# Routing attention and its feed-forward block on one core: loads dealt out two a slot, and GpSimd's indirect transfers held by a matmul

## The chip, the core and the metric

The kernel runs on one core of a Trainium2 chip. Six things work at once on that core, each with its own queue of instructions, taken in order: TensorE (PE in the profile; PEld is its loading of weights), VectorE (DVE), ScalarE (ACT), GpSimd (POOL), SyncE (SP, which here only issues transfers), and the core's 16 DMA engines, which carry the transfers out. An instruction names the semaphore values that it waits for; until they are there, everything behind it in its queue stands too. The metric is the device time of one execution in microseconds (us); lower is better.

## The reference

```python
def _attn_ref(q, k, v, centroids):            # 4 batches, 8 heads, 768 tokens, 64 wide
    q_assign = np.argmax(np.einsum('bhsd,hcd->bhsc', q_n, c_n), axis=-1)   # 16 clusters
    k_assign = np.argmax(np.einsum('bhsd,hcd->bhsc', k_n, c_n), axis=-1)
    mask = q_assign[:, :, :, None] == k_assign[:, :, None, :]
    scores = scale * np.matmul(q, k.transpose(0, 1, 3, 2))
    scores = np.where(mask, scores, -1000000000.0)
    attn = softmax(scores)                    # written out in the original
    return np.matmul(attn, v)

def _moe_ref(x, w_in, w_out, alpha):          # x: 3072 tokens by 512
    h = x @ w_in                              # 512 by 2048
    g = np.maximum(h, 0.0) + alpha * np.minimum(h, 0.0)
    return g @ w_out                          # 2048 by 512
```

A query attends only to the keys of its own cluster; q_n, k_n and c_n are q, k and the centroids divided by their norms. The heads' results side by side are x.

## The kernel before

The unit of attention is a pair: two heads of one batch. There are 16 pairs, n = 0 to 15. Pairs 0 to 8 score all keys against all queries and mask. Pairs 9 to 15 are sorted by cluster first: GpSimd scatters their rows of q, k and v to a scratch tensor in DRAM in the order of the clusters (order_scatter, an indirect transfer whose row numbers lie in the tile off), SyncE reads them back sorted (order_load), only blocks near the diagonal are scored, and GpSimd scatters the results back to the tokens' own order (put_back), from where SyncE fetches them (fetch_back).

Time goes by steps, u = 0 to 74. The steps up to 23 are the first part. From step 24 on (the second part, from about 195 us; 51 steps to about 800 us, so 12 us each on average) each pair or half pair has three steps, s = 0 to 2. A step has five slots; in the first step of a pair the score and weigh block (score, invert, weigh or weigh_near, mask, normalise, score again) takes the place of the first three, and two slots follow. In each slot the code writes out, in this order: tick (pieces that have come due: put_back is one), one piece of the attention's sums, the scatters that scatters_at allows, feed (one product of the feed-forward block, taken from the deque ffn: hidden, L1079, or final, L1097), and prepare (the work for later pairs: order_features, order_blocks and others). This order of the code is the order of each engine's queue. The pieces of ffn are what TensorE does between two blocks.

Two things set when transfers start. A load (load, load_v, order_load, fetch_back) is written out whole at the start of its step: eight transfers of 96 KB for q and k of a pair (tile qk), one or two for v (tile vt). SyncE issues them as soon as their buffer is free. GpSimd's indirect transfers (168 scatters, L688, and 84 put-backs, L1024) are paced by a handed number: pace() writes a 1x1 copy into ScalarE's queue (L664, tile pace, 8 buffers) and a 1x1 copy of that into GpSimd's (L665), so that GpSimd gets there only when ScalarE has come to that place in its own queue. A slot's scatters have one such pair of copies ahead of the first, each put-back has one of its own.

The scatters read their rows from two stage tiles in turn, which order_stage (L674) fills from q, k and v by three transfers on SyncE's queue, once the scatters of the tile's last use are done.

Of the kernel before, what the change touches and what calls it, by code (L numbers as in the profile page):

```python
# [23 lines left out]
def kernel(  # L24
# [77 lines left out]


    pairs = [(b, hp) for b in range(B) for hp in range(NCH)]
    NO = WHOLE * NCH - 3
# [9 lines left out]
    def load(n):  # L115

        b, hp = pairs[n]
        for w, src in enumerate((q, k)):  # L120
            raw = inp.tile([P, 2, NJ, D], FP32, name="qk")
            if n < 2:
                nc.sync.dma_start(
                    out=raw.rearrange("p h j d -> p h (j d)"),
                    in_=src[b, 2 * hp:2 * hp + 2].rearrange("h (p j) d -> p h (j d)",
                                                            j=NJ))
            elif n < NCH:
                for h in range(2):
                    nc.sync.dma_start(
                        out=by_token(raw)[:, :, h * D:(h + 1) * D],  # L130
                        in_=src[b, 2 * hp + h].rearrange("(p j) d -> p j d", j=NJ))
            for h in range(2):
                rows = src[b, 2 * hp + h]
                for x in range(D // Q if n >= NCH else 0):
                    r = h * D + x * Q
                    nc.sync.dma_start(
                        out=raw.rearrange("p h j d -> p (h j d)")[r:r + Q, :].rearrange(
                            "p (t i) -> p t i", i=Q),
                        in_=rows[:, x * Q:(x + 1) * Q].rearrange("(t p) i -> p t i", p=Q))
            raw_qk[n, w] = raw  # L140

    def load_v(n):
# [3 lines left out]
        if n < NCH:  # L146
            nc.sync.dma_start(out=vt.rearrange("p h j d -> p h (j d)"),
                              in_=rows.rearrange("h (p j) d -> p h (j d)", j=NJ))
        else:
            nc.sync.dma_start(out=vt.rearrange("p h j d -> p (h j) d"),  # L150
                              in_=rows.rearrange("h (j p) d -> p (h j) d", p=P))
        vts[n] = vt

# [353 lines left out]
    def second_part():  # L507

        first_part.close()
        for name, bufs in (("emore", 1), ("ordc", 1), ("ordp", 1), ("order", NP - NO),  # L510
                           ("xmore", 1), ("byrow", 1), ("pace", 8)):
            sorts[name] = fast.enter_context(tc.tile_pool(name=name, bufs=bufs))
# [3 lines left out]
    def order_constants():  # L516
# [23 lines left out]
        shift = ordc.tile([P, 2], FP32, name="shift")  # L540
        sorts["paced"] = ordc.tile([1, 1], FP32, name="paced")

# [136 lines left out]
    def order_scatter(n, i, x):  # L679
# [8 lines left out]
        nc.gpsimd.indirect_dma_start(  # L688
            out=scratch[n][1][h * NX + xx],
            out_offset=bass.IndirectOffsetOnAxis(ap=ranks[n][:, xx, h:h + 1], axis=0),  # L690
            in_=sorts["stage"][i % STAGES][:, x, :], in_offset=None,
            element_offset=h * 2 * S * P)

    def order_load(n):
# [3 lines left out]
            "p (h j d) -> p h j d", h=2, d=1)  # L698
        for h in range(2):
            r0 = 2 * h * S  # L700
            nc.sync.dma_start(out=found[:, h], in_=whole.bitcast(I32)[
                r0:r0 + S, D:D + 1].rearrange("(j p) d -> p j d", p=P))
        orders[n] = found
        for w in range(2):
            raw = inp.tile([P, 2, NJ, D], FP32, name="qk")
            for h in range(2):
                r0 = (2 * h + w) * S
                for x in range(D // Q):
                    r = h * D + x * Q
                    nc.sync.dma_start(  # L710
                        out=raw.rearrange("p h j d -> p (h j d)")[r:r + Q, :].rearrange(
                            "p (t i) -> p t i", i=Q),
                        in_=whole[r0:r0 + S, x * Q:(x + 1) * Q].rearrange(
                            "(t p) i -> p t i", p=Q))
            raw_qk[n, w] = raw
        vt = vpool.tile([P, 2, NJ, D], FP32, name="vt")
        for h in range(2):
            r0 = (2 * h + 1) * S
            nc.sync.dma_start(out=vt[:, h], in_=whole[r0:r0 + S, D:2 * D].rearrange(
                "(j p) d -> p j d", p=P))  # L720
        vts[n] = vt

# [298 lines left out]
    def put_back(to, place, rows, i):  # L1021
        j, h = divmod(i, 2)
        pace()
        nc.gpsimd.indirect_dma_start(  # L1024
            out=to[i],
            out_offset=bass.IndirectOffsetOnAxis(ap=place[:, h, j:j + 1], axis=0),
            in_=rows[j // HJ][:, j % HJ, h * D:(h + 1) * D], in_offset=None, element_offset=h * S * D)

    def fetch_back(n, whole):

        b, hp = pairs[n]
        raw = inp.tile([P, 2, NJ, D], FP32, name="qk").rearrange("p h j d -> p (h j d)")
        for h in range(2):
            for x in range(D // Q):
                r = h * D + x * Q
                nc.sync.dma_start(
                    out=raw[r:r + Q, :].rearrange("p (t i) -> p t i", i=Q),
                    in_=whole[h * S:(h + 1) * S, x * Q:(x + 1) * Q].rearrange(
                        "(t p) i -> p t i", p=Q))
# [22 lines left out]
    def ffn_pieces(b, half):  # L1062
# [12 lines left out]
        def hidden(f):  # L1075
            convert_up_to((f // FQ + 1) * (NCH + FQ) - FQ)
            ps = ps_f.tile([P, 512], FP32, name="fps")
            for c in range(NCH):
                nc.tensor.matmul(out=ps[:, 0:HS],  # L1079
                                 lhsT=w_in_sb[:, c, f * P:(f + 1) * P],  # L1080
                                 rhs=xTs[b, half][:, c, :],
                                 start=(c == 0), stop=(c == NCH - 1))
            slopes()
# [6 lines left out]
        def final(i, f0, on, off):  # L1090
# [5 lines left out]
            for f in range(f0, f0 + FQ):  # L1096
                nc.tensor.matmul(out=ps[:, 0:DM], lhsT=gs[f][:, i * P:(i + 1) * P],  # L1097
                                 rhs=w_out_sb[:, f, :], start=on and f == f0,
                                 stop=off and f == f0 + FQ - 1)
            if off:  # L1100
# [427 lines left out]
    todo = deque()  # L1528
    for u in range(TOGETHER, NS + 1):
        for piece in load_at.get(u, []):  # L1530
# [53 lines left out]
        for i in slots:  # L1584
# [19 lines left out]
    assert not prep_at and not todo  # L1604
    while due:
        tick()
        if due:
            tick()
# [222 lines left out]
```

## Time and profile before

| | before |
|---|---|
| median of three timed runs | 960.9 us (960.55 to 964.36) |
| profiled execution | 961.2 us, of which the profile's span is 959.3 |
| TensorE busy | 927.1 us, 97% of the span |
| VectorE, GpSimd, ScalarE busy | 656.2, 385.5 and 261.9 us |
| mean granted TensorE clock | 0.986 of full speed |

The profile is one execution; its time is the span and 1.9 us around it. TensorE's granted clock has two levels, 1.2 and 2.4 GHz, shown as 0.5 and 1.0; a value between them is a mean over a stretch. A time in brackets in a row is the idle time of the engine ahead of that instruction, with what ended it.

### The profile page before, as it was taken

The page shows a single profiled execution, that of the slowest core. Times are in us where ns is not written, and L with a number is a line of the kernel's source. Part 1 is how long each engine was busy: PE and PEld are TensorE (multiplying, and loading weights), DVE is VectorE, ACT ScalarE, POOL GpSimd, SP SyncE. Part 2 cuts the span into 40 slices and gives each one's busy share as a digit, 9 for nine tenths or more (in the row PEclk, how much of TensorE's full clock was granted, in tenths as well). Part 3 has the DMA queues.
Part 4 walks back from the last instruction along what each step waited for, and adds up shares of the span by engine and source line. Part 5 has one row for each costly group of instructions (what it writes and reads, how often), then busy time and mean ns, then how long its engine had stood idle before and what let it go on. Part 6 is the DMA issues. An engine that isn't in the chain of part 4 may idle for free.

```text
span 959.3 us, 11845 instructions
## 1 busy us (share of the span) xinstructions
PE 927.1 (97%) x3891; PEld 496.7 (52%) x3891; DVE 656.2 (68%) x1246; ACT 261.9 (27%) x660; POOL 385.5 (40%) x579
## 2 busy tenths in 40 slices
PE   8899999999999999999899999989899999999997
PEld 5434444445454444454454544545445454556886
DVE  5897798799498678798877988753446244598200
ACT  5664543322123221232223232112203120121000
POOL 2422222210036578477736777657615272000000
PEclk9999999999999999999999999999799999999999
DMA  9433757048002555155824353652421012000000
GB/s 287 141 114 105 146 117 141 17 92 161 0 14 80 138 118 123 39 117 124 164 49 66 51 106 99 135 105 64 70 56 26 11 35 57 1 1 0 23 23 26
DMA packets 231892, 77.71 MB, mean 81 GB/s; under 512 B 216960, under 2 KB 219728, under 8 KB 231824
## 3 DMA queue, kind: packets, MB, share of 16 engines
q1 hardware_dynamic: 222912, 62.72, 30.6%
q0 software_dynamic: 8064, 13.78, 4.5%
q8 instruction: 33, 0.54, 0.2%
q10 hardware_dynamic: 848, 0.39, 0.2%
q14 instruction: 35, 0.29, 0.1%
HBM read 52.25 MB, written 24.25 MB: 80 GB/s over the span
## 4 chain that ended last, share of the span: by engine, by line
PE 88%; DVE 3%; another core or an unknown queue 3%; ACT 2%; issue 2%; DMA 1%; SPq 0%; POOL 0%; ACTq 0%; DVEq 0%; POOLq 0%
PE fps L1079 25%; PE fps L1097 25%; PE sps L797 7%; PE vps L952 6%; PE sps L1315 4%; PE sps L1259 4%; PE fps L797 2%; PE vps L1259 2%; PE vps L1315 2%; PE mps L985 1%; PE fps L1315 1%; PE fps L1259 1%; PE vps L985 1%; PE sps L806 1%
## 5 line engine op out<-in xcount | busy, mean ns | idle before, releaser
L1079 PE MATMUL fps<-xT,w_in_sb 128*128 128x384 f32 x768 | 262.5, 495 | 8.3 <-ACT more L815 6.2
L1097 PE MATMUL fps<-w_out_sb,gT 128*128 128x512 f32 x576 | 254.1, 595 | 0.3 <-DVE gT L1071 0.3
L688 POOL DMA_INDIRECT scratch<-stage,off x168 | 178.4, 1062 | 64.5 <-issue 30.4
L1079 PEld LDWEIGHTS fps<-xT,w_in_sb 128*128 128x128 f32 x768 | 143.8, 192 | 113.6 <-ACT more L815 9.8
L1097 PEld LDWEIGHTS fps<-w_out_sb,gT 128*128 128x128 f32 x576 | 107.5, 190 | 132.2 <-issue 121.9
L665 POOL COPY paced<-pace 1x1 f32<-1x1 f32 x204 | 53.8, 264 | 166.7 <-ACT pace L664 164.7
L1085 ACT COPY gT<-fps 128x384 f32<-128x384 f32 x96 | 45.9, 478 | 240.7 <-PE fps L1079 185.4
L1071 DVE SCALAR_TENSOR_TENSOR gT<-gT,alpha 128x384 f32<-128x384 f32 x96 | 61.5, 649 | 69.1 <-ACT gT L1085 58.3
L1024 POOL DMA_INDIRECT back<-rows,off x84 | 87.0, 1036 | 22.8 <-issue 18.0
L797 PE MATMUL sps<-qkT 64*128 64x384 f32 (+1 forms) x464 | 87.2, 491 | 0.5 <-issue 0.5
L818 ACT ACTIVATE E<-sps 128x768 f32<-128x768 f32 (+1 forms) x76 | 56.4, 787 | 62.7 <-PE sps L806 42.6
L797 PEld LDWEIGHTS sps<-qkT 64*128 64x128 f32 x464 | 42.2, 188 | 39.6 <-issue 16.6
L838 DVE SCALAR_TENSOR_TENSOR more<-aq,key,more 128x384 f32<-128x384 bf16 (+2 forms) x116 | 60.4, 579 | 0.6 <-ACT more L815 0.6
L952 PE MATMUL vps<-E,vt 128*64 128x384 f32 x292 | 54.2, 495 | 0.0
L280 POOL TENSOR_TENSOR w_in_sb<-w_in_sb,power 128x512 f32<-128x512 f32 x16 | 24.0, 1502 | 68.6 <-DVE w_in_sb L277 68.6
L920 DVE RECIPROCAL inverses<-mps 64x12 f32<-64x12 f32 (+1 forms) x42 | 10.5, 251 | 52.9 <-PE mps L907 43.3
L280 POOL TENSOR_TENSOR w_out_sb<-w_out_sb,power 128x512 f32<-128x512 f32 x16 | 22.9, 1430 | 58.3 <-DVE w_out_sb L277 58.3
L838 DVE SCALAR_TENSOR_TENSOR E<-aq,key,E 128x384 f32<-128x384 bf16 (+2 forms) x88 | 45.1, 570 | 0.1
L848 DVE TENSOR_TENSOR acc<-acc,E 128x768 f32<-128x768 f32 x35 | 33.3, 951 | 14.5 <-ACT E L818 13.6
L1103 ACT COPY y<-fps 128x512 f32<-128x512 f32 x18 | 10.5, 586 | 99.2 <-PE fps L1097 86.8
L1105 DVE TENSOR_TENSOR y<-y,fps 128x512 f32<-128x512 f32 x24 | 16.4, 683 | 28.2 <-PE fps L1097 26.2
L797 PE MATMUL fps<-qkT 64*128 64x384 f32 (+1 forms) x136 | 31.0, 501 | 4.3 <-issue 3.6
(288 smaller groups left out, 1179.6 us busy)
## 6 DMA issues: line engine op xcount, KB each, us to landing
raw<-in_moe_w_in_dram SPq DMA_DIRECT2D x16, 512.0 KB
raw<-in_moe_w_out_dram SPq DMA_DIRECT2D x16, 512.0 KB
out_dram<-y SPq DMA_DIRECT2D x21, 256.0 KB
qk<-scratch SPq DMA_DIRECT2D x56, 96.0 KB
qk<-in_q_dram SPq DMA_DIRECT2D x48, 96.0 KB
qk<-in_k_dram SPq DMA_DIRECT2D x48, 96.0 KB
w_in_kept<-w_in_sb SPq DMA_DIRECT2D x8, 512.0 KB
vt<-in_v_dram SPq DMA_DIRECT2D x9, 384.0 KB
```

The costliest lines, as they stand in the source:

```text
L665: nc.gpsimd.tensor_copy(out=sorts["paced"], in_=token)
L688: nc.gpsimd.indirect_dma_start(out=scratch[n][1][h * NX + xx], out_offset=bass.IndirectOffsetOnAxis(ap=ranks[n][:, xx, h:h + 1], axis=0), ...
L797: nc.tensor.matmul(out=bank(ps, h, m), lhsT=qkT[r:r + D, S + c * P:S + (c + 1) * P], rhs=qkT[r:r + D, tokens], start=True, stop=not early_ ...
L818: nc.scalar.activation(out=E[:, :, 0:m], in_=ps[:, :, 0:m], func=AF.Exp, scale=SCALE)
L838: nc.vector.scalar_tensor_tensor(out=e, in0=of, scalar=keys[n][:, NJ + c, h:h + 1], in1=e, op0=ALU.is_equal, op1=ALU.mult)
L952: nc.tensor.matmul(out=po[r:r + D, 0:HS], lhsT=vts[n][:, h, c, :], rhs=e[:, h, :], start=(c == 0), stop=(c == NJ - 1))
L1024: nc.gpsimd.indirect_dma_start(out=to[i], out_offset=bass.IndirectOffsetOnAxis(ap=place[:, h, j:j + 1], axis=0), in_=rows[j // HJ][:, j % ...
L1071: nc.vector.scalar_tensor_tensor(out=gs[f], in0=gs[f], scalar=alpha[:, f:f + 1], in1=gs[f], op0=ALU.mult, op1=ALU.max)
L1079: nc.tensor.matmul(out=ps[:, 0:HS], lhsT=w_in_sb[:, c, f * P:(f + 1) * P], rhs=xTs[b, half][:, c, :], start=(c == 0), stop=(c == NCH - 1))
L1097: nc.tensor.matmul(out=ps[:, 0:DM], lhsT=gs[f][:, i * P:(i + 1) * P], rhs=w_out_sb[:, f, :], start=on and f == f0, stop=off and f == f0 + ...
L1259: nc.tensor.matmul(out=bank[to], lhsT=w_in_form(m, x, cc), rhs=rhs[:, cc, :], start=start and cc == 0, stop=cc == KH - 1, skip_group_check ...
L1315: nc.tensor.matmul(out=bank[to], lhsT=g_form(m, x, t), rhs=w_out_form(n, x), start=start and x == 0, stop=x == NQ - 1, skip_group_check=no ...
```

## The change

It has two parts. First, pace() and its two copies go. Each indirect transfer of GpSimd's waits instead for mark[0], the feed-forward matmul that was written out last; in a slot the scatters stand ahead of feed, so that this is the product of the slot before. Second, in the second part a load isn't written out whole at the start of its step. Its transfers go into a deque, loading, and deal(2) writes out two in each slot, each with a wait for mark[0]. A load counts as there (raw_qk, vts and orders are set) when its last transfer is written out; the row numbers (off) come last of a sorted pair's load, where they were first. turn_back, which reads what fetch_back fetched, comes 5 slots after the last of its transfers was written out, where it came 7 after the whole fetch (3 for 4 in the last pair). The loads of the first part, the stage loads (order_stage), the stores of w_in_kept and those of y are as before.

```diff
+    loading, mark, dealing = deque(), [None], []
+    def dealt(pieces, done):
+        loading.extend((1, piece) for piece in pieces)
+        loading.append((0, done))
+        if not dealing:
+            deal(len(loading))
+    def deal(room):
+        while loading and room >= loading[0][0]:
+            count, piece = loading.popleft()
+            piece()
+            room -= count
+    def paced(ins):
+        tc.add_manual_dep(
+            ins.ins, mark[0].ins.name,
+            mybir.DependencyInfo(mybir.DependencyClass.Sync, mybir.DependencyReason.DATA),
+            reason="paced")
+    def transfer(out, in_):
+        dma = nc.sync.dma_start(out=out, in_=in_)
+        if dealing:
+            paced(dma)
...
-    def pace():
-        token = sorts["pace"].tile([1, 1], FP32, name="pace")
-        nc.scalar.copy(token, ones[0:1, 0:1])
-        nc.gpsimd.tensor_copy(out=sorts["paced"], in_=token)
...
-        nc.gpsimd.indirect_dma_start(
+        paced(nc.gpsimd.indirect_dma_start(
             out=scratch[n][1][h * NX + xx],
...
     def put_back(to, place, rows, i):
         j, h = divmod(i, 2)
-        pace()
-        nc.gpsimd.indirect_dma_start(
+        paced(nc.gpsimd.indirect_dma_start(
...
-        later(4 if n == NP - 1 else 7, turn_back)
+            lambda: later(3 if n == NP - 1 else 5, turn_back))
...
-                nc.tensor.matmul(out=ps[:, 0:HS],
+                mark[0] = nc.tensor.matmul(out=ps[:, 0:HS],
...
             todo.popleft()()
+            deal(2)
             room = scatters_at(u - start_of[NO, None], s, i)
-            if room and sorting:
-                pace()
             while sorting and room:
...
-    while due:
+    while due or loading:
         tick()
+        deal(2)
```

On GpSimd's queue, at the first scatters of the first sorted pair, before: each slot's transfers follow a copy that waits for ScalarE (Activation), and the transfers themselves wait for nothing or for their stage load (the DMAHW semaphores).

```order
L685 COPY stage_1727<-number 64x4
L688 DMA scratch_2118<-stage_1727,off 3072x128 [waits DMAHW6_49,DMAHW7_49,DMAHW5_49,Pool_49]
L665 COPY paced<-pace 1x1 [waits Activation_49]
L688 DMA scratch_2118<-stage_1727,off 3072x128
L665 COPY paced<-pace 1x1 [waits Activation_49,Pool_49]
L688 DMA scratch_2118<-stage_1727,off 3072x128
L665 COPY paced<-pace 1x1 [waits Activation_49,Pool_49]
L688 DMA scratch_2118<-stage_1727,off 3072x128
```

The same place in the changed kernel:

```order
L707 COPY stage_1720<-number 64x4
L710 DMA scratch_2114<-stage_1720,off 3072x128 [waits DMAHW6_49,DMAHW7_49,DMAHW5_49,Pool_49]
L710 DMA scratch_2114<-stage_1720,off 3072x128 [waits PE_49]
L710 DMA scratch_2114<-stage_1720,off 3072x128
L710 DMA scratch_2114<-stage_1720,off 3072x128 [waits PE_49]
```

The copies are gone, the first transfer of a slot waits for TensorE (PE), and the second of the same slot has nothing more to wait for.

On SyncE's queue, at the load of q and k of a pair that is to be sorted, while another is being sorted, before: eight transfers of the load stand together behind the stage loads.

```order
L674 DMA stage_1727<-in_q_dram 64x4x64 [waits DMASW7_49,DMASW6_49,DMAHW7_49,DMASW5_49,DMASW4_49]
L674 DMA stage_1727<-in_k_dram 64x4x64 [waits DMAHW0_49]
L674 DMA stage_1727<-in_v_dram 64x4x64 [waits DMAHW1_49]
L136 DMA qk<-in_q_dram 32x24x32 [waits DVE_49,PE_49]
L136 DMA qk<-in_q_dram 32x24x32
L136 DMA qk<-in_q_dram 32x24x32 [waits DMAHW2_49]
L136 DMA qk<-in_q_dram 32x24x32 [waits DMAHW3_49]
L136 DMA qk<-in_k_dram 32x24x32 [waits DMAHW4_49,DVE_49,PE_49]
L136 DMA qk<-in_k_dram 32x24x32 [waits DMAHW5_49]
L136 DMA qk<-in_k_dram 32x24x32 [waits DMAHW6_49]
L136 DMA qk<-in_k_dram 32x24x32 [waits DMAHW7_49]
```

The same load in the changed kernel:

```order
L127 DMA qk<-in_q_dram 32x24x32 [waits DMAHW0_49,DVE_49,PE_49]
L127 DMA qk<-in_q_dram 32x24x32 [waits DMAHW1_49]
L696 DMA stage_1719<-in_q_dram 64x4x64 [waits DMASW3_49,DMASW2_49,DMAHW2_49,DMASW1_49,DMASW0_49]
L696 DMA stage_1719<-in_k_dram 64x4x64 [waits DMAHW3_49]
L696 DMA stage_1719<-in_v_dram 64x4x64 [waits DMAHW4_49]
L127 DMA qk<-in_q_dram 32x24x32 [waits DMAHW5_49]
L127 DMA qk<-in_q_dram 32x24x32 [waits DMAHW6_49]
L1125 DMA out_dram<-y 128x512 [waits DMAHW7_49,DVE_49]
L127 DMA qk<-in_k_dram 32x24x32 [waits DMAHW0_49,PE_49]
L127 DMA qk<-in_k_dram 32x24x32 [waits DMAHW1_49]
L127 DMA qk<-in_k_dram 32x24x32 [waits DMAHW2_49]
L127 DMA qk<-in_k_dram 32x24x32 [waits DMAHW3_49]
```

The load now comes in twos, with a stage load and a store of y between them, and a stage load that stands behind two of its transfers stands behind their wait for TensorE too (DMASW are the semaphores of GpSimd's transfers). On TensorE's queue nothing moves but two rows in the last steps.

## Rows read from the trace of the kernel before

**Rows 1.** The page: busy time, share of the span and instructions of each engine.
```profile
PE 927.1 (97%) x3891; PEld 496.7 (52%) x3891; DVE 656.2 (68%) x1246; ACT 261.9 (27%) x660; POOL 385.5 (40%) x579
```
**Rows 2.** Stretch, us: busy us of PE, PEld, DVE, ACT, POOL; PEclk, DMA share, GB/s.
```profile
320.00:680.00 360.00, 340.39 (x1340) 173.78 (x1339) 269.30 (x505) 91.69 (x304) 242.87 (x367) 0.98 0.45 96
```
**Rows 3.** Timeline of TensorE, late matmuls: start, us, instruction, [idle before].
```profile
358.80 1.84 PE L1079 MATMUL fps<-xT,w_in_sb 128*128 128x384 f32 x3 [1.91 <-ACT E L815]
...
423.15 2.20 PE L1079 MATMUL fps<-xT,w_in_sb 128*128 128x384 f32 x6 [1.52 <-ACT more L815]
...
479.32 2.29 PE L1079 MATMUL fps<-xT,w_in_sb 128*128 128x384 f32 x3 [2.50 <-ACT more L815]
...
562.14 2.20 PE L1079 MATMUL fps<-xT,w_in_sb 128*128 128x384 f32 x6 [2.13 <-ACT more L815]
...
613.93 0.26 PE L457 MATMUL mps<-cluster,spread 128*128 128x24 bf16 x4 [1.22 <-DVE begins L623]
...
635.62 2.20 PE L985 MATMUL mps<-more,vt 128*64 128x384 f32 x8 [2.89 <-DVE inverses L920]
...
677.01 1.43 PE L797 MATMUL fps<-qkT 64*128 64x320 f32 x2 [2.15 <-issue]
679.91 1.43 PE L797 MATMUL fps<-qkT 64*128 64x320 f32 x2 [1.47 <-issue]
```
**Rows 4.** Stretches around four of these, columns as in rows 2.
```profile
356.00:366.00 10.00, 8.09 (x26) 4.51 (x23) 7.65 (x13) 2.96 (x8) 6.62 (x10) 0.83 0.49 162
...
474.00:484.00 10.00, 7.00 (x28) 3.38 (x26) 4.10 (x10) 2.31 (x5) 3.71 (x7) 0.83 1.00 192
...
632.00:642.00 10.00, 7.11 (x41) 4.09 (x38) 7.05 (x17) 4.16 (x11) 1.07 (x2) 0.83 0.59 93
674.00:688.00 14.00, 10.38 (x48) 5.11 (x46) 5.73 (x13) 3.62 (x12) 8.13 (x13) 0.63 0.45 71
```
**Rows 5.** Timeline of ScalarE: L815 in a late block and in one on time.
```profile
358.25 0.87 ACT L815 ACTIVATE E<-fps 128x384 f32<-128x384 f32 x2 [6.82 <-PE sps L797]
...
395.31 0.87 ACT L815 ACTIVATE more<-fps 128x384 f32<-128x384 f32 x2 [4.19 <-PE fps L797]
```
**Rows 6.** Stretches that end at such blocks' L815, and two others; columns as in rows 2.
```profile
222.50:231.00 8.50, 8.50 (x50) 3.96 (x50) 7.18 (x14) 3.28 (x7) 0.00 (x0) 1.00 0.88 167
349.90:358.40 8.50, 6.99 (x42) 3.01 (x38) 4.39 (x10) 1.68 (x5) 6.62 (x13) 1.00 1.03 224
...
553.10:561.60 8.50, 6.91 (x42) 3.01 (x38) 5.67 (x14) 1.58 (x6) 6.49 (x11) 1.00 0.98 175
...
443.90:452.40 8.50, 8.50 (x48) 4.08 (x48) 4.58 (x11) 2.01 (x4) 6.03 (x11) 1.00 0.85 174
...
630.00:636.00 6.00, 3.11 (x26) 1.73 (x24) 1.10 (x3) 1.82 (x4) 2.43 (x5) 0.98 0.29 78
675.00:681.00 6.00, 2.52 (x4) 1.00 (x4) 0.62 (x1) 2.64 (x9) 4.00 (x7) 0.64 0.10 33
```
**Rows 7.** GpSimd's groups by line, 279 to 800 us: busy us, mean ns, idle before.
```profile
L688 POOL DMA_INDIRECT scratch<-stage,off x168 | 178.4, 1062 | 64.5 <-issue 30.4 <-DMA stage<-in_v_dram 20.5 <-POOL stage L685 4.2
L1024 POOL DMA_INDIRECT back<-rows,off x84 | 87.0, 1036 | 22.8 <-issue 18.0 <-ACT pace L664 3.8 <-DVE acc L886 0.5
L665 POOL COPY paced<-pace 1x1 f32<-1x1 f32 x203 | 53.2, 262 | 106.4 <-ACT pace L664 104.4 <-issue 1.4
```
**Rows 8.** The page: the hidden products, whole run.
```profile
L1079 PE MATMUL fps<-xT,w_in_sb 128*128 128x384 f32 x768 | 262.5, 495 | 8.3 <-ACT more L815 6.2
```
**Rows 9.** Timeline: the last load that is sorted from, and its reader.
```profile
560.62 1.91 SPq L136 DMA_DIRECT2D qk<-in_k_dram  x4
...
573.13 0.96 DVE L580 STREAM_TRANSPOSE qk<-qk 128x768 f32<-128x768 f32 x1
```
**Rows 10.** Timeline: the last fetch's reader, and TensorE behind it.
```profile
804.60 1.04 DVE L1043 STREAM_TRANSPOSE xT<-qk 128x384 f32<-128x384 f32 x2 [6.76 <-DMA qk<-back]
...
808.15 1.45 PE L1259 MATMUL sps<-xT,w_in_sb 128*128 128x384 f32 x4
```

More of the change, by code (lines that the diff above doesn't have):

```diff
@@ L135, in load @@
                     r = h * D + x * Q
-                    nc.sync.dma_start(
-                        out=raw.rearrange("p h j d -> p (h j d)")[r:r + Q, :].rearrange(
+                    pieces.append(lambda raw=raw, r=r, rows=rows, x=x: transfer(
+                        raw.rearrange("p h j d -> p (h j d)")[r:r + Q, :].rearrange(
                             "p (t i) -> p t i", i=Q),
-                        in_=rows[:, x * Q:(x + 1) * Q].rearrange("(t p) i -> p t i", p=Q))
-            raw_qk[n, w] = raw
+                        rows[:, x * Q:(x + 1) * Q].rearrange("(t p) i -> p t i", p=Q)))
+            dealt(pieces, lambda n=n, w=w, raw=raw: raw_qk.update({(n, w): raw}))
     def load_v(n):
@@ L148, in load_v @@
                               in_=rows.rearrange("h (p j) d -> p h (j d)", j=NJ))
+            vts[n] = vt
         else:
-            nc.sync.dma_start(out=vt.rearrange("p h j d -> p (h j) d"),
-                              in_=rows.rearrange("h (j p) d -> p (h j) d", p=P))
-        vts[n] = vt
+            dealt([lambda: transfer(vt.rearrange("p h j d -> p (h j) d"),
+                                    rows.rearrange("h (j p) d -> p (h j) d", p=P))],
+                  lambda: vts.update({n: vt}))
     cen = const.tile([P, D], FP32, name="cen")
@@ L698, in order_load @@
             "p (h j d) -> p h j d", h=2, d=1)
[L699 to L703, printed above, removed]
         for w in range(2):
             raw = inp.tile([P, 2, NJ, D], FP32, name="qk")
+            pieces = []
             for h in range(2):
@@ L709, in order_load @@
                     r = h * D + x * Q
-                    nc.sync.dma_start(
-                        out=raw.rearrange("p h j d -> p (h j d)")[r:r + Q, :].rearrange(
+                    pieces.append(lambda raw=raw, r=r, r0=r0, x=x: transfer(
+                        raw.rearrange("p h j d -> p (h j d)")[r:r + Q, :].rearrange(
                             "p (t i) -> p t i", i=Q),
-                        in_=whole[r0:r0 + S, x * Q:(x + 1) * Q].rearrange(
-                            "(t p) i -> p t i", p=Q))
-            raw_qk[n, w] = raw
+                        whole[r0:r0 + S, x * Q:(x + 1) * Q].rearrange(
+                            "(t p) i -> p t i", p=Q)))
+            dealt(pieces, lambda n=n, w=w, raw=raw: raw_qk.update({(n, w): raw}))
         vt = vpool.tile([P, 2, NJ, D], FP32, name="vt")
[L717 to L721, printed above, removed]
+        dealt([lambda h=h: transfer(
+            vt[:, h], whole[(2 * h + 1) * S:(2 * h + 2) * S, D:2 * D].rearrange(
+                "(j p) d -> p j d", p=P)) for h in range(2)], lambda: vts.update({n: vt}))
+        dealt([lambda h=h: transfer(found[:, h], whole.bitcast(I32)[
+            2 * h * S:(2 * h + 1) * S, D:D + 1].rearrange("(j p) d -> p j d", p=P))
+            for h in range(2)], lambda: orders.update({n: found}))
     def order_blocks(n, w):
@@ L1032, in fetch_back @@
         raw = inp.tile([P, 2, NJ, D], FP32, name="qk").rearrange("p h j d -> p (h j d)")
[L1033 to L1039, printed above, removed]
+        dealt([lambda h=h, x=x: transfer(
+            raw[h * D + x * Q:h * D + (x + 1) * Q, :].rearrange("p (t i) -> p t i", i=Q),
+            whole[h * S:(h + 1) * S, x * Q:(x + 1) * Q].rearrange("(t p) i -> p t i", p=Q))
+            for h in range(2) for x in range(D // Q)],
+            lambda: later(3 if n == NP - 1 else 5, turn_back))
         def turn_back():
@@ L1096, in final @@
             for f in range(f0, f0 + FQ):
-                nc.tensor.matmul(out=ps[:, 0:DM], lhsT=gs[f][:, i * P:(i + 1) * P],
-                                 rhs=w_out_sb[:, f, :], start=on and f == f0,
-                                 stop=off and f == f0 + FQ - 1)
+                mark[0] = nc.tensor.matmul(
+                    out=ps[:, 0:DM], lhsT=gs[f][:, i * P:(i + 1) * P],
+                    rhs=w_out_sb[:, f, :], start=on and f == f0,
+                    stop=off and f == f0 + FQ - 1)
             if off:
```

16 lines of the change are left out of this document (9 added, 7 removed).

## The prediction

> **What bounds the kernel now.** I read the page first: TensorE is busy for 97% of the span [rows 1], so only its gaps, its clock or its work can pay, and the change leaves its work alone. Next I read the stretches. From 320 to 680 us, where GpSimd's indirect transfers run, TensorE is busy for 340.4 of 360 us: 19.6 us of gaps [rows 2]. The timeline of TensorE has most of them in eight places; those that I show sum to 15.8 us [rows 3]. In the row of a gap one reads who ended it: mostly ScalarE (L815, the exponentials of a block). A gap has a second price. In the 10 us around the gaps at 358.8, 479.3 and 635.6 us the mean granted clock is 0.83, and around 677 us it is 0.63 over 14 us [rows 4]. The levels being 1.0 and 0.5, that is 0.17 x 10 = 1.7 us lost three times, and 0.37 x 14 = 5.2 us once: 10.3 us. Gaps and clock make about 30 us, the most that anything can win here.
>
> So the question is why ScalarE is late. In the timeline L815 follows 4.19 us of idle time in a block that is on time, 6.82 in a late one, where the releaser is a product of TensorE's that had ended before [rows 5]. Its own queue is not full (27% busy), so ScalarE was told late. I then laid 8.5 us stretches ahead of L815 side by side [rows 6]. The late blocks (at 358, 423, 479 and 562 us; the first and the last of the four are shown) have two things together: GpSimd is issuing indirect transfers for 6.5 us or more of 8.5, and the DMA engines' share is 0.98 or more. The block at 231 us has a DMA share of 0.88 and no indirect transfer, and no gap; that at 452 us has 6.03 us and 0.85, and no gap. The stretches at 630 and 675 us are late with a DMA share of 0.29 and 0.10, while GpSimd is in or just behind a train of such transfers. I take it that a train of indirect transfers delays what waits for TensorE, and that full DMA engines make it worse. This is inferred from times alone.
>
> **The pace copies (first part).** 203 copies of 262 ns leave GpSimd's queue, 53 us [rows 7], and as many leave ScalarE's. Both lie beside TensorE's work; ScalarE is busy for 27% and GpSimd for 40% [rows 1], so by themselves they are worth 0. Only where a transfer itself is waited for would a removed copy give back its 0.26 us, and no row shows TensorE waiting for one.
>
> **The hold by a product.** Two scatters of a slot cost GpSimd 2 x 1.06 us [rows 7], and a product of the feed-forward block takes TensorE 262.5 us / 96 = 2.7 us [rows 8] (96 products of eight matmuls), so a slot can take its scatters, and with a put-back of 1.04 us it just can't. GpSimd therefore keeps up while scatters run alone, and still falls behind where put-backs run too (600 to 700 us). A transfer whose product is long done starts at once, so a backlog runs as a train as before; the hold only stops transfers from running ahead. Behind the waiting transfer on GpSimd stand only other transfers and the small copies of the stage's numbers. I give the gap at 635.6 us half (its train is scatters alone): (2.9 + 1.7) / 2 = -2.3, with bounds of 0 and -4.6. The pair of gaps at 677 and 680 us stays: 0, with a bound of -(2.15 + 1.47 + 5.2) = -8.8.
>
> **The loads in twos.** Before, eight transfers of 96 KB are issued in some 4 us (four in 1.91 [rows 9]) at the start of a step, and where the step begins with a block, they fill the DMA engines during it. After, two go out in a slot, 192 KB in some 2.7 us, and none inside a score and weigh block, since a block has no deal(2). That takes the second of the two conditions away from all four late blocks. Their gaps are 1.91 + 1.52 + 2.50 + 2.13 = 8.1 us and two of them cost 1.7 us of clock each. I count three of the four, without that at 562 us, whose train is of put-backs, which the hold leaves: 1.91 + 1.52 + 2.50 + 2 x 1.7 = -9.3. Bounds: -11.5 (all) and 0. The gap at 613.9 us stands in a burst of sorted loads too: -1.2, with a bound of 0.
>
> The Trainium skill speaks against this (SBUF — State Buffer, Who interferes with whom): a DMA never contends with a compute engine, having ports of its own. By that rule spreading loads gives 0 and the sum would lose its largest term. The trace agrees as far as the block at 231 us goes, and not with the difference between the late blocks and that at 452 us, which is small.
>
> **What the hold makes late.** Dealt loads end later. The last q and k that are sorted from are issued by 562.5 us, and read at 573.1 [rows 9]; eight in four slots of 2.7 us and a block between end about 10 us later, so the transpose L580 slips by some 2 us and VectorE's queue with it, in which the slopes of the products stand. I take +1.5, bounds 0 and +3 for this place. Sorted loads (ten transfers and two of numbers) are written out three or four steps of 12 us ahead, and six slots are a step and a bit: covered, 0; if one were late, VectorE would hold TensorE for up to two slots, +5. The stage loads stand behind dealt loads on SyncE's queue and wait with them; GpSimd already waits 20.5 us for stage loads [rows 7] and TensorE does not wait for it, so 0, but the backlog behind such a wait is a train: +1, bounds 0 and +3. The last fetch is dealt over two rounds and turned two slots sooner; its reader waited 6.76 us and TensorE runs on 3.55 us behind it [rows 10] without a gap in front: 0, bounds -1 and +3.
>
> **The sum.** -9.3 - 2.3 - 1.2 + 1.5 + 1 = -10.3 us against the profiled execution's 961.2, which lies 0.3 above the median: 950.9, say 951. The bounds sum to -27 and +14, which no one run would reach together.
>
> **The rivals.**
> *Nothing nets.* The delay comes from the train itself, and 252 transfers at (178.4 + 87.0 + 53.2) / 252 = 1.26 us each, their copies included [rows 7], are as many as before; break a train here and it stands there. For it: the two stretches with a low DMA share. Against it: 6.03 us of GpSimd without a gap at 452 us. Then only small terms are left: -2.3 + 2.5, 961, between 957 and 965. The Trainium skill's rule on ports, above, would end here as well, at 961.
> *Slower: the held loads come late.* SyncE's queue is in order, so a transfer that waits for a product also holds the stage loads behind it, and GpSimd's scatters and a pair's whole chain (scatter, load, L726, score) shift by the slots lost. It decides from the point where a pair's sorted load ends later than its turn, three steps after it is written out. Each such pair stalls TensorE for one to two slots; of seven pairs, three would cost 3 x 4 = 12 us, less 3 for what is gained anyway: 970, between 966 and 978. The Trainium skill's rule that one should issue a DMA early and wait on its semaphore late (DMA: Bandwidth & Descriptors, Rules for kernel authors) points the same way; no row here shows such a stall.
> *More: the trains go altogether.* If a product's mark keeps every train short, the gaps at 635.6, 677 and 680 us go with their clock too: -11.5 - 4.6 - 8.8 - 1.2 + 2.5 = -23.6, 938, between 934 and 944. Against it: the backlog of put-backs, which no mark holds.
>
> **How the numbers follow.** I give the forecast 0.45 (944 to 956 its own range), more 0.14, nothing 0.24, slower 0.17. The predicted time is the forecast's, 951. For 8 in 10 the range leaves out the lower half of "more" and most of "slower", and reaches from 939 to 966. Half a per cent is 4.8 us, about what a measurement of this kernel tells from no change. Below 956.1 lie the forecast and "more": 0.59. Within lie most of "nothing": 0.24. Above 965.7 lies "slower": 0.17.
>
> **What would show it.** In the changed kernel's trace: no DMA share near 1 in the stretch ahead of a block's L815, and ScalarE's idle time there about 4 us at the blocks near 358, 423 and 479 us; TensorE's gaps between 320 and 680 us down from 19.6 to about 12; the clock rows of 0.83 gone at the first two and the 0.63 near 677 us still there. The hold is right if GpSimd waits for TensorE where it waited for ScalarE, and its trains of scatters are shorter. I am wrong if the late blocks are late with few loads in flight (the train alone does it), if L580 or L726 waits for qk loads for more than 3 us, or if the gaps come back at other blocks.

## The result, and the profile after

The changed kernel took 972.1 us in the median of four executions (965.99 to 975.98) beside 961.1 us of the kernel before: 1.0117 times as long, with a 95% interval of 1.0081 to 1.0152. Its profiled execution, the fastest of the four, took 966.0 us, 4.8 more than that of before, so the profile shows less than half of the loss.

First the stretches of the changed kernel, columns as in [rows 2]:

```profile
320.00:680.00 360.00, 341.91 (x1343) 174.33 (x1341) 269.04 (x505) 79.46 (x159) 205.45 (x222) 0.98 0.44 96
680.00:800.00 120.00, 114.81 (x410) 60.80 (x411) 55.55 (x106) 20.53 (x43) 42.85 (x44) 0.97 0.19 40
```

TensorE's gaps from 320 to 680 us are 18.1 us, where they were 19.6; the forecast was about 12. Behind 680 us there are 5.2 us of gaps where there were none, which makes 23.3 us for 19.6 from 320 to 800 us. The copies are gone as planned (ScalarE 91.7 to 79.5 us, GpSimd 242.9 to 205.5). Next, the late matmuls in the timeline of TensorE that answer to [rows 3], and the stretches around them:

```profile
563.84 2.93 PE L1095 MATMUL fps<-xT,w_in_sb 128*128 128x384 f32 x4 [8.68 <-ACT more L834]
...
609.16 4.21 PE L1095 MATMUL fps<-xT,w_in_sb 128*128 128x384 f32 x6 [3.91 <-issue]
...
685.19 1.43 PE L816 MATMUL fps<-qkT 64*128 64x320 f32 x2 [5.65 <-ACT gT L1101]
...
558.00:572.00 14.00, 8.16 (x23) 4.79 (x24) 7.48 (x15) 3.23 (x6) 5.67 (x7) 0.76 0.31 65
606.00:618.00 12.00, 8.84 (x19) 5.01 (x20) 9.51 (x18) 1.43 (x3) 7.73 (x9) 0.72 0.80 181
680.00:694.00 14.00, 8.81 (x50) 4.92 (x51) 6.29 (x15) 3.76 (x8) 6.82 (x7) 0.76 0.25 52
```

The gaps at 358, 423 and 479 us are gone, as forecast, and so are those at 613.9 and 635.6 us. Three large ones, 18.2 us together, stand instead. Counted matmul by matmul, those at 564 and 685 us stand where there were gaps of 2.13 and 1.47 us (562 and 680 us in [rows 3]), and the one at 609 us stands where there was none. Each has a mean granted clock of 0.72 to 0.76 around it, which costs 0.24 x 14 = 3.4 us each time. That is 10.2 us together, and the clock cost 10.3 us before: what the profile shows of the loss is gaps, and the clock's price has only moved with them. The timeline of GpSimd, ScalarE and VectorE at the first of them (remote: the profile names no releaser):

```profile
541.14 1.09 POOL L1042 DMA_INDIRECT back<-rows,off  x1 [2.94 <-PE mps L486]
...
560.42 0.98 POOL L710 DMA_INDIRECT scratch<-stage,off  x1 [0.28 <-issue]
...
563.25 0.56 DVE L1071 TENSOR_TENSOR xT<-vps,rd 128x384 f32<-128x384 f32 x1 [9.39 <-remote]
563.29 0.87 ACT L834 ACTIVATE more<-fps 128x384 f32<-128x384 f32 x2 [13.59 <-remote]
```

VectorE and ScalarE wait for products of TensorE's that had begun at 552.5 and 553.0 us, and both go on at 563.3. GpSimd issued 15 indirect transfers without a pause over 1 us from 541.1 to 561.4 us; the wait ends 1.9 us behind the last. The trace's own record of TensorE's semaphore says what came late. Five of the matmuls that raise it ended between 553.0 and 555.2 us; the record has no rise between 548.82 and 563.23 us, and then five within 0.2 us. Whether the products were late too, or only the signal, it can't tell, since the ends of matmuls are modelled. The other two gaps also stand behind trains, of 13 and 15 transfers, that end at 606.5 and 682.2 us; TensorE goes on 2.7 and 3.0 us later.

### The profile page after: what moved, and what is told of

Same layout as the page of the kernel before. It is cut to its first block, busy times and chain, and to the rows that moved or that the text cites. A ratio compares the mean times of both kernels' runs of the same rounds, so it can differ in the third digit from the quotient of the medians.

```text
span 964.2 us, 11365 instructions
## 1 busy us (share of the span) xinstructions
PE 927.1 (96%) x3891; PEld 497.2 (52%) x3891; DVE 656.6 (68%) x1246; ACT 245.2 (25%) x456; POOL 331.2 (34%) x375
## 4 chain that ended last, share of the span: by engine, by line
PE 88%; DVE 4%; another core or an unknown queue 3%; DMA 2%; issue 2%; ACT 1%; ACTq 0%; SPq 0%; DVEq 0%
PE fps L1095 26%; PE fps L1113 26%; PE sps L816 7%; PE vps L971 6%; PE sps L1332 4%; PE sps L1276 4%; PE fps L816 2%; PE vps L1332 2%; PE vps L1276 2%; PE vps L1004 1%; PE mps L1004 1%; PE fps L1276 1%; PE fps L1332 1%; DMA vt<-in_v_dram 1%
## 5 line engine op out<-in xcount | busy, mean ns | idle before, releaser
L710 POOL DMA_INDIRECT scratch<-stage,off x168 | 180.8, 1076 | 179.1 <-DVE acc L867 64.2
L1042 POOL DMA_INDIRECT back<-rows,off x84 | 83.8, 998 | 128.7 <-issue 33.9
L867 DVE TENSOR_TENSOR acc<-acc,E 128x768 f32<-128x768 f32 x35 | 33.3, 951 | 14.5 <-ACT E L837 13.6
L837 ACT ACTIVATE more<-sps 128x768 f32<-128x768 f32 (+1 forms) x40 | 29.3, 767 | 22.3 <-PE sps L816 16.5
```

The costliest lines, as they stand in the source:

```text
L710: paced(nc.gpsimd.indirect_dma_start(out=scratch[n][1][h * NX + xx], out_offset=bass.IndirectOffsetOnAxis(ap=ranks[n][:, xx, h:h + 1], axi ...
L837: nc.scalar.activation(out=E[:, :, 0:m], in_=ps[:, :, 0:m], func=AF.Exp, scale=SCALE)
L1042: paced(nc.gpsimd.indirect_dma_start(out=to[i], out_offset=bass.IndirectOffsetOnAxis(ap=place[:, h, j:j + 1], axis=0), in_=rows[j // HJ][: ...
```

## The experiments

The groups of runs fell on different chips. The kernel before takes 934 us on some and 956 to 961 on others, so that only ratios within a group compare. The two parts of the change and the whole, each beside the kernel before:

| | chip of 934 us | chips of 956 to 961 us |
|---|---|---|
| whole change | 1.0066 (1.0044 to 1.0088) | 1.0117, and 1.0142 (1.0102 to 1.0182) |
| first part alone (hold) | 0.9994 (0.9983 to 1.0005) | 1.0070 (1.0034 to 1.0107) |
| second part alone (dealt loads) | 1.0128 (1.0089 to 1.0168) | 1.0049 (1.0006 to 1.0092) |

**The parts, and the whole again (a chip of 934).** Theory A: GpSimd's trains hold up what TensorE tells the other engines, and the hold makes them worse. Theory B: dealt loads come late. The first part alone, its core:

```diff
     def dealt(pieces, done):
         loading.extend((1, piece) for piece in pieces)
         loading.append((0, done))
-        if not dealing:
-            deal(len(loading))
+        deal(len(loading))
     def transfer(out, in_):
         dma = nc.sync.dma_start(out=out, in_=in_)
-        if dealing:
-            paced(dma)
```

with the numbers off first and turn_back 7 slots behind, as before. The second part alone puts pace() and its two copies back ahead of a slot's scatters and of each put-back and takes paced() from GpSimd's transfers. A third kernel makes the transfers wait for the copy out of the product:

```diff
-            nc.scalar.copy(gs[f], ps[:, 0:HS])
+            copied[0] = nc.scalar.copy(gs[f], ps[:, 0:HS])
...
-            ins.ins, mark[0].ins.name,
+            ins.ins, (by or mark)[0].ins.name,
```

where by is copied for GpSimd's transfers, and where the copies and sums of y set copied[0] too.

The first part alone:

> Only the first part of the change: GpSimd's transfers wait for a product, loads are written out whole as before. Theory A (trains of indirect transfers hold up TensorE's semaphores; the hold lets the trains grow past 13 transfers): slower than before, 963 to 975, with one to three TensorE gaps of 4 us or more, each at the end of a train of 13 or more. Theory B (the dealt loads come late): about as before, 958 to 963, no gap over 3.5 us.

The second part alone:

> Only the second part: loads dealt two a slot behind a product, GpSimd's transfers paced by the handed copies as before. Theory A: as before or faster, 952 to 962, since the trains are those of the kernel before and the loads have left the blocks; the gaps at 358, 423 and 479 us gone. Theory B: slower, 966 to 975, with the large gaps of the changed kernel at about 563, 609 and 685 us.

Held by the copy:

> The changed kernel, but GpSimd's transfers wait for the copy of a product out of the bank (ScalarE's, or VectorE's sum) in place of the product. Theory A (trains): like the changed kernel, 964 to 976, gaps of 4 us or more at the end of long trains. Theory C (it is GpSimd's own waiting for TensorE's semaphore that disturbs it): as before or faster, 952 to 962, gaps under 3.5 us.

The whole once more:

> The changed kernel once more, for a second profile and its spread. If the large gaps come at fixed places of the program, they stand again within a few us of 563, 609 and 685 us. If they are a matter of chance in the timing, they stand at other trains, and the time is anywhere from 964 to 977.

Measured: 0.9994, 1.0128, 1.0082 (1.0065 to 1.0099) and 1.0066. Here theory B is right and theory A isn't. Theory C can't be judged, since on this chip nothing was late behind a train; waiting for the copy costs no less than waiting for the product. The whole shows how a dealt load costs, in the timelines of SyncE, VectorE and TensorE and in two stretches:

```profile
558.59 1.11 SPq L127 DMA_DIRECT2D qk<-in_q_dram  x2
559.80 2.40 SPq L127 DMA_DIRECT2D qk<-in_k_dram  x4
...
564.80 0.98 DVE L608 STREAM_TRANSPOSE qk<-qk 128x768 f32<-128x768 f32 x1 [0.57 <-DMA qk<-in_k_dram]
...
572.30 0.97 DVE L745 STREAM_TRANSPOSE qkT<-qk 128x768 f32<-128x768 f32 x1
...
573.32 2.40 PE L816 MATMUL sps<-qkT 64*128 64x224 f32 x8 [3.01 <-DVE qkT L745]
...
570.00:584.00 14.00, 10.41 (x33) 4.78 (x34) 12.33 (x24) 2.23 (x4) 8.57 (x10) 0.63 0.35 97
...
320.00:680.00 360.00, 354.03 (x1417) 181.48 (x1417) 280.73 (x532) 84.59 (x170) 213.96 (x227) 0.99 0.45 99
```

The load that answers to [rows 9] stands in the deque behind the last two transfers of a sorted load and on both sides of a block. VectorE waits 0.57 us for it behind 3.77 us of other idle time, and its transpose comes at 564.8, where the first part alone has it at 562.85. Everything behind it in VectorE's queue slips too: qkT is turned at 572.3 for 570.3, TensorE stands for 3.0 us, and the clock behind that gap (0.63 over 14 us) takes 0.37 x 14 = 5.2 us. Together that is 8.2 us; the profiled executions are 5.3 us apart (942.2 and 936.9), the medians 7.6. The Trainium skill has the rule (DMA: Bandwidth & Descriptors, Rules for kernel authors): issue a DMA early, wait on its semaphore late. This place bears it out, with the clock as the larger part of the price. The second part alone costs more than the whole: VectorE stands 7.25 and 0.74 us ahead of this load's two transposes there, for 3.77 and 0.57 in the whole. Why the hold makes that milder no run shows.

The other thing to see on this chip is what is missing. First, in the first part alone, the stretch ahead of a block's second exponentials, ScalarE at them, and a stretch with a long train; then the same of another block in the second part alone:

```profile
542.30:550.80 8.50, 8.50 (x48) 4.07 (x48) 8.40 (x21) 2.76 (x5) 6.41 (x7) 1.00 1.07 176
...
550.81 0.87 ACT L831 ACTIVATE more<-fps 128x384 f32<-128x384 f32 x2 [4.19 <-PE fps L813]
...
538.00:571.00 33.00, 33.00 (x130) 16.23 (x129) 32.24 (x58) 7.52 (x16) 26.24 (x27) 1.00 0.62 109
```

```profile
409.90:418.40 8.50, 8.50 (x48) 4.05 (x48) 8.38 (x19) 2.76 (x5) 7.47 (x12) 1.00 0.93 185
...
418.43 0.87 ACT L841 ACTIVATE more<-fps 128x384 f32<-128x384 f32 x2 [4.19 <-PE fps L823]
```

A train of 23 transfers in 33 us runs through a block, and ScalarE waits 4.19 us there, the time of a block without a stall [rows 5]. GpSimd at 6.41 of 8.5 us with a DMA share of 1.07, and at 7.47 us with 0.93, cost nothing; the prediction's two conditions were 6.5 us and 0.98. So neither a train nor full DMA engines are enough by themselves: the late semaphores need something that some chips have and this one hasn't.

**One load undone, four a slot, no hold (a chip of 959).** One kernel writes the eight transfers of the late load out whole; one deals four a slot; one takes the hold off both kinds of GpSimd's transfers (the scatters are shown):

```diff
+            if n == NP - 1:
+                for piece in pieces:
+                    piece()
+                raw_qk[n, w] = raw
+                continue
             dealt(pieces, lambda n=n, w=w, raw=raw: raw_qk.update({(n, w): raw}))
...
-            deal(2)
+            deal(4)
...
-        paced(nc.gpsimd.indirect_dma_start(
+        (nc.gpsimd.indirect_dma_start(
```

The load whole:

> The changed kernel with one load undone: q and k of the last pair to be sorted (the one whose transpose L608 came 2 us late) are written out whole at the start of their step. Theory B (that one late load, its gap at 573 us and the clock behind it are the loss on the chip of the first group): as the kernel before there, 932 to 936, no gap at 573 us and no clock of 0.5 behind it. If dealing costs at many places: 938 to 942.

Four a slot:

> The changed kernel with four transfers a slot in place of two. Theory B: the load of the last pair is issued before the block, so no gap at 573 us: 932 to 936 on a chip where the kernel before takes 934. Where TensorE's semaphores come late (the chip of the first profile) I expect less than the changed kernel's loss, but no gain.

No hold:

> The changed kernel without any hold on GpSimd's transfers: each runs when its stage load or its rows are there. Theory A (long trains hold up TensorE's semaphores): the trains grow, and gaps of 3 us or more stand at their ends: 8 us or more above the changed kernel. Theory B (trains alone do nothing, the late load does): as the changed kernel, within 3 us.

Measured: 1.0124 (1.0087 to 1.0161), 1.0181 (1.0114 to 1.0248) and 1.0350 (1.0269 to 1.0430). The changed kernel wasn't in this group; on two other chips of this kind it took 1.0117 and 1.0142. Beside these, undoing the late load shows no gain: TensorE stands for 8.65 us at 562.4 us anyway, while the load arrives. Four a slot shows none either (TensorE stands for 6.1, 4.7 and 5.1 us at 566, 594 and 612 us); I had expected less than the changed kernel's loss, and have no cause. Without a hold the loss was the largest, as theory A says, though a second try, below, has a smaller one. The kernel before, profiled in this group:

> The kernel before, for a profile on this chip. On a chip where it takes 934 us: none of the late blocks at 358, 423, 479 and 562 us, no gap at 636 and 677 us, though trains of 12 to 16 transfers and DMA shares near 1 stand ahead of blocks as in the first profile. On one where it takes 961: the gaps are at the same trains again.

It took 1.0018 (0.9979 to 1.0056) and has its gaps again at 358, 421, 628 and 674 us (1.7, 1.4, 2.8 and 4.9 us). It has none over 1.3 us at the blocks near 479 and 562 us, so that a gap that is missing from one profile proves little.

**The parts again, and spacing (a chip of 961).** Two more kernels put a 1x1 copy that waits for nobody ahead of each transfer, in the changed kernel and in the first part alone:

```diff
+        nc.gpsimd.tensor_copy(out=sorts["paced"], in_=ones[0:1, 0:1])
         paced(nc.gpsimd.indirect_dma_start(
```

The first part:

> The first part alone, again, since the first group ran on a chip where the kernel before takes 934 us and shows no late semaphore. On a chip where it takes 955 to 962, theory A (trains without the pace copies between their transfers hold up TensorE's semaphores longer) says 1.005 to 1.02 times the kernel before, with gaps of 4 us or more at the end of trains of 13 or more. Theory B (dealing is the loss) says 1.00. On a chip of 934: 1.00 either way.

The second part:

> The second part alone, again. On a chip of 955 to 962, theory A says under 1.008, gaps at block ends under 3.5 us but for one near 680 us; theory B says 1.01 to 1.02. On a chip of 934: 1.013, as in the first group.

The changed kernel, spaced:

> The changed kernel with a 1x1 copy, waiting for nobody, on GpSimd's queue ahead of each of its 252 transfers: only their spacing changes, from 1.3 to about 1.6 us. On a chip of 955 to 962, theory A2 (it is the closer spacing that made the trains worse) says no gap over 4 us at a train's end and 0.99 to 1.005; if the length of a train in transfers decides, it is as the changed kernel, 1.01. On a chip of 934: 1.007 either way, the late load.

The first part, spaced:

> The first part alone with the same copies ahead of each transfer. Theory A2: as the kernel before or faster, 0.985 to 1.003, since the late load is gone too. If spacing does nothing: as the first part alone in this group.

Measured: 1.0070 and 1.0049 (table), 1.0066 (1.0024 to 1.0109) and 1.0020 (0.9985 to 1.0055). Each part costs. In the first part alone the spacing gives back half a per cent at the most (the intervals overlap); the changed kernel without it wasn't in this group. The gaps move rather than go: with spacing the first part alone stands for 5.1, 3.7 and 3.5 us at 557, 637 and 679 us, among others. What this group does settle is which part took the gaps at 358 and 423 us away. ScalarE at these two blocks and the stretches ahead of them, first in the first part alone, then in the second:

```profile
354.63 0.87 ACT L831 ACTIVATE E<-fps 128x384 f32<-128x384 f32 x2 [2.75 <-PE fps L813]
...
415.70 0.87 ACT L831 ACTIVATE more<-fps 128x384 f32<-128x384 f32 x2 [4.19 <-PE fps L813]
...
346.10:354.60 8.50, 8.50 (x48) 4.04 (x48) 6.34 (x14) 2.84 (x5) 4.61 (x6) 1.00 0.69 178
407.20:415.70 8.50, 8.50 (x48) 4.08 (x48) 8.38 (x19) 2.76 (x5) 5.28 (x6) 1.00 0.43 112
```

```profile
358.35 0.87 ACT L841 ACTIVATE E<-fps 128x384 f32<-128x384 f32 x2 [6.62 <-PE sps L823]
...
420.82 0.87 ACT L841 ACTIVATE more<-fps 128x384 f32<-128x384 f32 x2 [6.25 <-PE sps L823]
...
349.90:358.40 8.50, 7.29 (x44) 3.19 (x40) 4.31 (x10) 1.89 (x5) 6.91 (x13) 1.00 0.70 173
412.30:420.80 8.50, 7.72 (x46) 3.40 (x42) 7.42 (x18) 2.27 (x4) 7.19 (x13) 1.00 1.00 205
```

With the loads written out whole and the transfers held, both blocks are on time (2.75 and 4.19 us). With the loads dealt and the transfers paced as before, both are late (6.62 and 6.25). At the second block GpSimd's time and the DMA share differ together. The first tells the two apart: the share is 0.69 and 0.70 there, and GpSimd is busy for 4.61 us where the block is on time and for 6.91 us where it is late. It is the hold that took these gaps away, by leaving GpSimd less to do ahead of the block; dealing did nothing for them. And the block at 418.4 us above, the same one as that at 420.8 us in the same kernel, was on time on a chip of 934.

The new gap at 564 us comes with the hold as well. The first part alone has it, with whole loads:

```profile
531.14 0.96 POOL L1039 DMA_INDIRECT back<-rows,off  x1 [7.81 <-DVE E L854]
...
541.41 1.10 POOL L1039 DMA_INDIRECT back<-rows,off  x1 [2.93 <-PE mps L483]
...
564.35 5.49 PE L1092 MATMUL fps<-xT,w_in_sb 128*128 128x384 f32 x8 [4.62 <-ACT more L831]
```

A put-back that is held waits for its product, and what is behind it on GpSimd with it: GpSimd stands for 7.8 and 2.9 us ahead of these two. How much of that is the hold's alone the rows don't tell; the first names a piece of VectorE's, which ended 0.1 us behind a rise of TensorE's semaphore. What was put off runs as a train of 15 to 561.4 us, through the block: it ends 13.7 us behind the block's first exponentials, at 547.7, where in the kernel before the train of this place ended 8.1 us behind them (552.3 and 560.4).

**Trains broken by pauses (a chip of 934).** Eight such copies ahead of every fourth transfer, in the first part alone and in the kernel before:

```diff
+        sent[0] += 1
+        if sent[0] % 4 == 0:
+            for _ in range(8):
+                nc.gpsimd.tensor_copy(out=sorts["pause"], in_=ones[0:1, 0:1])
```

The first part:

> The first part alone, with a pause on GpSimd's queue ahead of every fourth transfer (eight 1x1 copies that wait for nobody, some 2.6 us), so that no train is longer than four. Theory A (the length of a train without a pause decides whether TensorE's semaphores come late): on a chip of 955 to 962, no gap of 3 us or more at a block's end near 563, 610 and 685 us, and 0.985 to 1.003 times the kernel before if no sorted load comes late for it. If trains have nothing to do with it: 1.007 and the gaps stand. On a chip of 934 only what the pauses make late shows: 1.00 to 1.01.

The kernel before:

> The kernel before with the same pauses. Theory A on a chip of 955 to 962: the gaps at 358, 421, 636 and 677 us go, 0.975 to 0.995. Otherwise 1.00 to 1.01. On a chip of 934: 1.00 to 1.01.

Measured: 1.0438 (1.0401 to 1.0476) and 1.0554 (1.0533 to 1.0575). On this chip they say nothing of the trains, and my 1.00 to 1.01 was far off. They price a late transfer instead, in the timelines of VectorE and TensorE of the first:

```profile
475.09 0.98 DVE L752 STREAM_TRANSPOSE qkT<-qk 128x768 f32<-128x768 f32 x1 [15.76 <-DMA qk<-scratch]
...
478.94 2.40 PE L823 MATMUL sps<-qkT 64*128 64x224 f32 x8 [15.84 <-DVE mine L494]
```

A sorted load can't start before the pair's last scatter, and VectorE and TensorE stand for 16 us. Pauses are no way to break trains here: GpSimd has no such time to give. On a chip with late blocks these two weren't run.

**Held scatters, put-backs paced as before (a chip of 956).** If the hold takes gaps away where scatters run and makes them where put-backs do, it should be kept for scatters alone, with loads as before:

```diff
     def put_back(to, place, rows, i):
         j, h = divmod(i, 2)
-        paced(nc.gpsimd.indirect_dma_start(
+        pace()
+        (nc.gpsimd.indirect_dma_start(
```

in the first part alone, with pace() back. Beside it, no hold once more, and the changed kernel as the measure.

Mixed:

> Loads as before; the scatters held by a product (which took away the gaps at 358, 421 and 479 us in the first part alone), the put-backs paced by the handed copies as before (whose trains cost less than the held ones). On a chip of 955 to 962, theory A: 0.985 to 0.997 times the kernel before. On a chip of 934: 1.00.

No hold:

> No hold on any transfer of GpSimd's, again. On a chip of 955 to 962: 1.03 to 1.045, gaps at the ends of trains of 16 to 24, as before. On a chip of 934, if trains do nothing there: as the changed kernel there, 1.005 to 1.012, with no gap at a train's end; if trains matter there too once they are long enough: 1.02 or more.

The changed kernel:

> The changed kernel on the chip of this group, as the measure for the two others: 1.007 on a chip of 934 (the late load at 573 us), 1.008 to 1.015 on one of 955 to 962 (gaps of 4 us or more near 563 and 685 us).

Measured: 0.9959 (0.9926 to 0.9992), 1.0186 (1.0136 to 1.0235) and 1.0142 (1.0102 to 1.0182). No hold is under the 1.03 that I had expected at the least, and its interval overlaps that of the changed kernel. The trains through the block near 560 us in the three, first without a hold, then mixed; the stretch of the train, and TensorE behind it:

```profile
542.40:574.80 32.40, 25.41 (x109) 13.31 (x105) 19.76 (x37) 6.03 (x12) 25.44 (x28) 0.89 0.44 90
...
567.31 2.93 PE L1095 MATMUL fps<-xT,w_in_sb 128*128 128x384 f32 x4 [6.97 <-issue]
```

```profile
540.60:553.40 12.80, 12.80 (x66) 6.34 (x64) 11.66 (x25) 4.08 (x13) 11.34 (x17) 1.00 1.02 165
...
554.47 2.85 PE L1100 MATMUL fps<-xT,w_in_sb 128*128 128x384 f32 x8 [0.99 <-ACT more L838]
```

Without a hold, 24 transfers run until 574.8 us and TensorE stands for 7.0 us; here it goes on before the train's end, which the picture of a wait for the last transfer doesn't explain. In the changed kernel of this group it stands for 5.5 us at 560.6, and mixed for 1.0 us, since the put-backs start at 528.6 us and the last part of their train, nine transfers, is over at 553.4. The version was run once more, in five rounds on the same chip:

> The held scatters with put-backs paced by the handed copies, again, in five rounds. On a chip of 955 to 962: 0.992 to 0.999 once more if the gain was real, 1.00 if it was the spread. On a chip of 934: 0.998 to 1.003.

Measured: 0.9964 (0.9930 to 0.9998). So on this chip mixed is 0.4% faster than the kernel before, with intervals that end just under 1, and 1.8% faster than the changed kernel. Large gaps have not gone altogether: its two profiles have one of 6.1 us at 631 us and one of 7.6 us at 598 us. On a chip of 934 it wasn't run.

## Why the prediction was wrong

**Right:** that the gaps at 358 and 423 us go, and in the first profile that at 479 us too (its block is still late there, with 5.96 us of idle time on ScalarE, and another profile of the changed kernel has 1.7 us of gap); that the DMA share ahead of these three blocks falls (0.55 to 0.71, from 1.00 to 1.03); that the pair at 677 us stays (5.7 us at 685 us, for 3.6); that the copies by themselves are worth about 0, as far as a chip of 934 tells, where taking them out for the hold made 0.9994; that GpSimd's trains belong to the late blocks, on the chips that have late blocks; that L580 would be late.

**Wrong: the loads in twos, -9.3.** This step failed in its cause. It put the gaps down to full DMA engines and gave dealing the credit. With dealing alone they stayed; with the hold alone those at 358 and 423 us went, and near the place of that at 479 us one of 2.5 us was left (468 us). The stretches I had laid side by side [rows 6] held both causes at once, so they could not tell them apart, and the block with a DMA share of 0.88 and no transfer pointed the right way. On a chip of 934 both together did nothing.

**Wrong: the hold by a product.** I wrote that it only stops transfers from running ahead, gave its term no worse bound than 0 and counted -2.3. But work that can't run ahead runs later: the train of held put-backs ends some 6 us later against its block than that of the paced ones. There the gap grew from 2.1 to 8.7 us, with 3.4 us of clock that it had not cost before (the granted clock was 1.00 from 558 to 572 us in the kernel before). Put-backs paced as before made it 1.0 us, beside 5.5 of the changed kernel in that group. Another gap, of 3.9 us, came behind a train at 609 us. The gap of 635.6 us did go in the first profile, but it is 3.7 and 4.0 us in two other profiles of held kernels.

**Mis-sized: what the hold makes late, +1.5 for L580.** Where nothing hides it, it cost 3.0 us of gap and 5.2 us of clock. I had left the clock out, though the rows of before showed that each gap of 2.5 us or more is followed by 1.7 us or more of it. On the chips with late blocks the price seems to be hidden in the stall at the same place: undoing the load made 1.0124 there, beside 1.0117 and 1.0142 of the whole on two others.

**The rivals.** "Slower" ended nearest (forecast 966 to 978), by luck: held loads that come late cost something only on a chip of 934, and its sorted loads were late nowhere but in the kernels with pauses. "Nothing nets" had the sentence that held: break a train here and it stands there.

**Open:** what on some chips holds up TensorE's semaphores while GpSimd issues its transfers. The three large gaps all stand behind trains, and on other chips 23 in a row cost nothing. That longer trains cost more is not shown: no hold took 1.0186 and 1.0350 in two groups, and the one with the changed kernel beside it doesn't tell them apart. Nor does a run show how much of the whole's 1.0142 is trains and how much the load.

## What to carry to other kernels

When two possible causes lie in the same stretches of a trace, don't price the change by one of them: look for a stretch that has only one, and if there is none, keep both signs open. Pacing an engine that is behind with its work doesn't remove the work; ask where the postponed part will run and what is waiting there. Price a stall of TensorE with the clock behind it, and compare only on one chip.

## What was not expected of the hardware

One and the same program took 934 us on some chips and 956 to 961 on others. Matmul by matmul, the changed kernel's profile on the chip of 961 is 1.1 to 1.2 us behind that on the chip of 934 up to 450 us, and 24.1 us behind from 680 us on: the difference is stalls and the clock behind them, all in the stretch where GpSimd's indirect transfers run in trains. On the slower chips VectorE and ScalarE were seen waiting 9.4 and 13.6 us for TensorE while it had nothing left to do, and both went on together 1.9 us behind the train's last transfer; in the kernel without a hold TensorE went on before a train's end.

The traces differ in one more thing. In all 14 profiles from the slower chips, TensorE's semaphore rises in bunches between 200 and 800 us (three times or more, each within 0.1 us of the last, 4 to 9 such bunches a profile); in none of the six from chips of 934 does it do so once. And of the 11,008 rises that sixteen for each of the kernel's 688 transfers make, the traces from chips of 934 have 10,906 to 10,981, those from the others 6,107 to 7,003. So the chips differ in how semaphores are carried, or in how the profiler records them. Whether the recording takes part in the stalls no run here shows.
